# Four new fill-up tiles and one larger one shift where the operands of the expert stage begin in SBUF

## The chip, the cores and the metric

The kernel runs on one core of one Trainium2 chip. The metric is the device time of one execution in microseconds. The kernel before was timed in 3 runs; a further execution was taken with the hardware profiler.

## The reference, cut to what matters

Attention gives 4608 rows of 512 numbers, and a mixture of 8 experts is applied to them. The logits pick one expert per row; the expert is two matrix products with a ReLU between:

```python
out_up = np.repeat(sm_attn(q_d, k_d, v_d), 4, axis=2)      # coarse attention over means of 4 positions
out_local = ...                                            # softmax over keys with |i - j| < 4
x = (out_up + out_local).transpose(0, 2, 1, 3).reshape(4608, 512)
expert_idx = np.argmax(x @ w_gate, axis=1)                 # 8 experts, gate_w = softmax probability
for e in range(8):
    h = np.maximum(x_sorted[lo:hi] @ w1[e], 0.0)           # 512 -> 1024
    y_sorted[lo:hi] = h @ w2[e]                            # 1024 -> 512
return gate_w[:, None] * y_sorted[inv_perm]
```

q, k and v are 8 batches x 8 heads x 576 positions x 64.

## The kernel before, in words

**Attention, to about 239 us.** 32 pairs of heads go through a hand-written list of steps, `PASS`. In it TensorE multiplies plain float32 operands (each such matmul stands in the trace as two) and transposes float32 tiles with the identity `ident` of the tile `cf`. Finished rows are scattered to a DRAM table `xs`, one region per expert.

**Experts, from about 239 us to the end** (expert 0 starts earlier, between the last steps of attention). Each operand is split in a high and a low part (`w1h`, `w1l`, `xh`, `xl`, `w2h`, `w2l`, `hh`, `hl`), all float32r, and a product is three matmuls: high by high, high by low, low by high. A matmul has a stationary operand, loaded into the array by a weight load of 128 columns (engine PEld in the trace), and a moving operand that streams through, mostly 512 columns.

- `s1(e, f)`, lines 587 to 600: for block f of 128 of the 1024 hidden units, 12 matmuls into one bank; stationary `w1` tiles, moving `xh0`/`xl0` (512 tokens). Expert 0 does it in two parts of 256 tokens.
- `s2(e, t)`, through `down`, lines 602 to 612: for a tile t of 128 tokens, 24 matmuls; stationary `hh`/`hl`, moving `w2`, 8 tiles f.
- The rows past 512 of an expert go through `full` (stationary `xh1`/`xl1` with moving `w1`, then stationary `thh`/`thl` with moving `w2`) or, when at most 64 are left, `half` (stationary `xb` and `tb`). In this data each of the two is run 4 times. Which one is decided on the chip by a count, in `rest_of`.

**Where tiles lie.** Every tile pool here keeps its tiles one behind the other in the order in which their names are first used, each size rounded up to a multiple of 32 bytes per partition. `wpool` and, behind it, `mp[0]` lie on the left and grow upward; `mp[1]` lies at the upper end of the right side and `wodd` below it, so what is added to one of them moves its first tiles down. A tile that is only there to take up room is made by `home`, which also writes zeros to it with a memset on GpSimd. The tiles that the matmuls read, all of sizes that are multiples of 256 bytes, begin at these addresses modulo 256:

| tiles | pool | before |
|---|---|---|
| `w1` of even experts | `wpool` | 224 |
| `xh0`, `xl0`, `hh`, `hl` | `mp[0]` | 224 |
| `w2`, f = 0 to 5 | `mp[0]` | 224 |
| `w2`, f = 6, 7; `xh1`, `xl1`, `xb`, `thh`, `thl`, `tb` | `mp[1]` | 224 |
| `w1` of odd experts | `wodd` | 224 |

The slices that matmuls take of them begin at multiples of 256 bytes too. So, in the kernel before, the distance modulo 256 from a moving to a stationary operand is 0 in each matmul of the expert stage. In attention the distances vary from matmul to matmul: the stationary `XT` of the transposes (line 444) begins at 64, 80, 96 and 112 for even pairs of batches and at 128 to 176 for odd ones, with the moving identity always at 0; the moving `AT` of line 337 begins at 32 or 64 for alternating pairs of heads and steps by 208 within them, with the stationary `vw` always at 96.

The engines' queues in the expert stage: ScalarE and VectorE split the next weights and evacuate banks, GpSimd casts the rows' indices and issues the indirect DMAs of the outputs (line 616), SyncE the loads.

## Time and profile before

| | |
|---|---|
| median of 3 runs | 669.18 us (665.74 to 670.09) |
| profiled execution | 662.55 us, of which the span of its instructions is 660.6 us |
| mean granted TensorE clock | 0.992 |
| TensorE matmuls busy | 625.5 us (95%) |
| weight loads busy (beside matmuls) | 510.3 us (77%) |
| VectorE, ScalarE, GpSimd busy | 371.9, 320.0, 216.3 us |

[...] How much time a matmul takes up is read from the starts of two that follow each other; this text calls that its pitch. Start times stand with two decimals of a microsecond, so a pitch is best read over many.

### The profile page before, as it was taken

Reading aid. Unit: us, or ns where it says so; the run is one execution under the profiler, and the core shown is the slowest. Engines: PE = TensorE matmul, PEld = TensorE weight load, DVE = VectorE, ACT = ScalarE, POOL = GpSimd, SP = SyncE. Lnnn points to the kernel's source line nnn. Section 1 sums busy time; section 2 is a strip of 40 time slices with the busy share of each in tenths; the row PEclk is TensorE's granted clock in tenths of the full one; section 3 lists DMA queues with packets and bytes.
Section 4 is the critical chain, followed back from the end, with each engine's and each line's share of the span. In section 5 each row is a group of like instructions: output and inputs, shape, how many; then the busy total and the mean of one; then the engine's idle time right before and its main releaser. Section 6 shows DMA issues by size and latency. Waiting matters only on the chain.

```text
span 660.6 us, 15650 instructions
## 1 busy us (share of the span) xinstructions
PE 625.5 (95%) x6163; PEld 510.3 (77%) x6163; DVE 371.9 (56%) x691; ACT 320.0 (48%) x845; POOL 216.3 (33%) x316
## 2 busy tenths in 40 slices
PE   7988998999998989999999999999999989999994
PEld 3766776777776978888888888888888878888873
DVE  5968899999996646382373065166128247115020
ACT  3656777778785535362362254254236145224120
POOL 6955887888770611101101011101110101110111
PEclk9989999999999989999999999999999999999998
DMA  9999999899534496284176238238228528110001
GB/s 305 286 270 264 291 280 279 261 281 269 170 128 124 150 297 193 63 232 147 52 182 187 66 133 233 65 94 216 99 80 224 178 77 209 48 46 1 33 18 41
DMA packets 66226, 108.52 MB, mean 164 GB/s; under 512 B 15388, under 2 KB 36524, under 8 KB 66112
## 3 DMA queue, kind: packets, MB, share of 16 engines
q1 hardware_dynamic: 59840, 87.62, 47.8%
q0 software_dynamic: 5984, 19.01, 7.9%
q8 instruction: 66, 1.08, 0.7%
q10 hardware_dynamic: 288, 0.42, 0.2%
q14 instruction: 48, 0.39, 0.2%
HBM read 86.98 MB, written 23.67 MB: 167 GB/s over the span
## 4 chain that ended last, share of the span: by engine, by line
PE 68%; issue 10%; DVE 10%; DMA 4%; POOL 3%; ACT 2%; SPq 1%; POOLq 0%; another core or an unknown queue 0%; DVEq 0%; ACTq 0%
PE p L596 8%; PE p L597 8%; PE p L595 8%; PE p L611 7%; PE p L609 7%; PE p L610 7%; PE pD L285 3%; PE pPV L337 2%; PE pX L322 2%; PE pX L691 2%; PE pX L710 2%; DMA vd<-in_vd_dram 2%; PE pPV L350 1%; DVE A L271 1%; PE pS L236 1%
## 5 line engine op out<-in xcount | busy, mean ns | idle before, releaser
L595 PE MATMUL p<-xh,w1h 128*128 128x512 f32 (+1 forms) x288 | 106.7, 370 | 3.2 <-issue 1.9
L616 POOL DMA_INDIRECT out_dram<-y,tix x39 | 38.0, 974 | 212.9 <-ACT y L628 201.5
L596 PE MATMUL p<-xl,w1h 128*128 128x512 f32 (+1 forms) x288 | 106.0, 368 | 0.8 <-DVE xl L543 0.8
L597 PE MATMUL p<-xh,w1l 128*128 128x512 f32 (+1 forms) x288 | 105.9, 368 | 0.0
L609 PE MATMUL p<-w2h,hh 128*128 128x512 f32 x256 | 101.1, 395 | 0.0
L611 PE MATMUL p<-w2h,hl 128*128 128x512 f32 x256 | 99.8, 390 | 0.0
L610 PE MATMUL p<-w2l,hh 128*128 128x512 f32 x256 | 99.6, 389 | 0.0
L600 DVE SCALAR_TENSOR_TENSOR hl<-p,hh 128x512 fp32r<-128x512 f32 (+1 forms) x72 | 45.5, 632 | 93.3 <-ACT hh L599 91.3
L599 ACT ACTIVATE hh<-p 128x512 fp32r<-128x512 f32 (+1 forms) x72 | 39.6, 551 | 78.9 <-PE p L597 78.9
L628 ACT ACTIVATE y<-p,gi 128x512 f32<-128x512 f32 x32 | 22.0, 689 | 93.8 <-PE p L611 89.4
L595 PEld LDWEIGHTS p<-xh,w1h 128*128 128x128 f32 x288 | 55.0, 191 | 13.1 <-issue 2.3
L596 PEld LDWEIGHTS p<-xl,w1h 128*128 128x128 f32 x288 | 55.1, 191 | 9.7 <-DVE xl L543 0.9
L597 PEld LDWEIGHTS p<-xh,w1l 128*128 128x128 f32 x288 | 55.0, 191 | 8.7
L611 PEld LDWEIGHTS p<-w2h,hl 128*128 128x128 f32 x256 | 48.0, 188 | 10.2
L610 PEld LDWEIGHTS p<-w2l,hh 128*128 128x128 f32 x256 | 48.1, 188 | 9.6
L609 PEld LDWEIGHTS p<-w2h,hh 128*128 128x128 f32 x256 | 48.1, 188 | 9.4
L471 POOL DMA_INDIRECT xs<-xr,ix x36 | 36.8, 1021 | 42.0 <-ACT w1h L181 12.4
L182 DVE TENSOR_TENSOR w1l<-raw,w1h 128x512 fp32r<-128x512 f32 (+1 forms) x72 | 49.4, 686 | 0.8
L299 ACT ACTIVATE AD<-pD,mxd 128x144 f32<-128x144 f32 x96 | 35.3, 376 | 19.1 <-DVE A L271 18.8
L543 DVE TENSOR_TENSOR xl<-pX,xh 128x512 fp32r<-128x512 f32 x38 | 24.7, 684 | 35.2 <-ACT xh L542 34.2
L585 DVE TENSOR_TENSOR w2l<-raw,w2h 128x512 fp32r<-128x512 f32 x64 | 43.4, 681 | 1.1 <-ACT w2h L584 0.6
L216 POOL TENSOR_TENSOR vdt<-vd 72x512 f32<-72x512 f32 x32 | 40.8, 1276 | 6.4 <-DMA vd<-in_vd_dram 4.2
(148 smaller groups left out, 1204.7 us busy)
## 6 DMA issues: line engine op xcount, KB each, us to landing
raw<-in_w_dram SPq DMA_DIRECT2D x64, 512.0 KB
qk<-in_qk_dram SPq DMA_DIRECT2D x32, 583.0 KB
vw<-in_vw_dram SPq DMA_DIRECT2D x32, 320.0 KB
vd<-in_vd_dram SPq DMA_DIRECT2D x32, 288.0 KB
xrow<-xs SPq DMA_DIRECT2D x32, 192.0 KB
xrow<-xs SPq DMA_DIRECT2D x32, 128.0 KB
xs<-zs SPq DMA_DIRECT2D x6, 512.0 KB
xs<-pad SPq DMA_DIRECT2D x3, 257.0 KB
```

What stands on the lines that cost most here:

```text
L182: nc.vector.tensor_sub(lo[:, s], src[:, s], hi[:, s])
L216: nc.gpsimd.tensor_add(t2, v[:, 0:2], v[:, 2:4])
L585: nc.vector.tensor_sub(lo, src, hi)
L595: nc.tensor.matmul(p, wh[:, fs], xh[:, k, r], start=(k == 0), stop=False)
L596: nc.tensor.matmul(p, wh[:, fs], xl[:, k, r], start=False, stop=False)
L597: nc.tensor.matmul(p, wl[:, fs], xh[:, k, r], start=False, stop=(k == 3))
L599: nc.scalar.activation(hh[:, f, r], p, AF.Relu)
L600: nc.vector.scalar_tensor_tensor(hl[:, f, r], p, 0.0, hh[:, f, r], op0=OP.max, op1=OP.subtract)
L609: nc.tensor.matmul(p, hh, wh, start=(f == 0), stop=False)
L610: nc.tensor.matmul(p, hh, wl, start=False, stop=False)
L611: nc.tensor.matmul(p, hl, wh, start=False, stop=(f == 7))
L616: ins = nc.gpsimd.indirect_dma_start(out=out, out_offset=bass.IndirectOffsetOnAxis(ap=ix, axis=0), in_=y, in_offset=None, bounds_check=N - ...
```

## The change

`home` gets the pool as an argument and is defined earlier. Four new fill-up tiles are made, and one grows:

- `gap2`, 64 bytes in `wpool` ahead of `w1h0`;
- `gap3`, 192 bytes at the head of `mp[0]`;
- `gap`, from 64 to 96 bytes in `mp[0]`, ahead of `w2`;
- `gap1`, 160 bytes behind the last tile of `mp[1]`;
- `gap4`, 64 bytes behind the last tile of `wodd`.

```diff
+    def home(name, n, pl):
+        nc.gpsimd.memset(pl.tile([128, n], F32, name=name), 0.0)
...
         if (e, k) not in W1:
             pl = wpool if e % 2 == 0 else wodd[0]
+            if (e, k) == (0, 0):
+                home("gap2", 16, wpool)
             W1[e, k] = (pl.tile([128, F], F32R, name=f"w1h{k}"), pl.tile([128, F], F32R, name=f"w1l{k}"))
+            if (e, k) == (1, 3):
+                home("gap4", 16, pl)
...
         if (e, f) == (0, 0):
-            home("tgi", 2)
-            home("ttix", 1)
-            home("gap", 16)
+            home("tgi", 2, mp[0])
+            home("ttix", 1, mp[0])
+            home("gap", 24, mp[0])
...
             mp["th", 1] = [mp[1].tile([128, 8, 2, HALF], F32R, name="tb")]
+            home("gap1", 40, mp[1])
...
             _, mp["p1"] = pool(name="psM1", bufs=2, space=PSUM)
+            home("gap3", 48, mp[0])
             x_load(0, 0)
```

No matmul, load or other instruction is added, removed or moved but the memsets of the four new tiles.

## Rows read from the trace of the kernel before

**Rows 1.** The page, part 1: engine, busy us (share of the span), instructions.

```profile
PE 625.5 (95%) x6163; PEld 510.3 (77%) x6163; DVE 371.9 (56%) x691; ACT 320.0 (48%) x845; POOL 216.3 (33%) x316
```

**Rows 2.** The chain of waits that ended last, by engine and by line.

```profile
PE 68%; issue 10%; DVE 10%; DMA 4%; POOL 3%; ACT 2%; SPq 1%; POOLq 0%; another core or an unknown queue 0%; DVEq 0%; ACTq 0%
PE p L596 8%; PE p L597 8%; PE p L595 8%; PE p L611 7%; PE p L609 7%; PE p L610 7%; PE pD L285 3%; PE pPV L337 2%; PE pX L322 2%; PE pX L691 2%; PE pX L710 2%; DMA vd<-in_vd_dram 2%; PE pPV L350 1%; DVE A L271 1%; PE pS L236 1%
```

**Rows 3.** A stretch, mostly expert 1: busy us by engine, granted clock, DMA share, GB/s.

```profile
268.00:313.00 45.00, 45.00 (x200) 37.24 (x200) 22.74 (x36) 19.66 (x35) 6.65 (x13) 1.00 0.52 149
```

**Rows 4.** Groups by line and shape, TensorE: count | busy us, mean ns | idle before.

```profile
L609 PE MATMUL p<-w2h,hh 128*128 128x512 f32 x256 | 101.1, 395 | 0.0
...
L595 PE MATMUL p<-xh,w1h 128*128 128x512 f32 x224 | 87.3, 390 | 1.9 <-issue 1.9
...
L595 PE MATMUL p<-xh,w1h 128*128 128x256 f32 x64 | 19.4, 304 | 1.3 <-ACT xh L542 1.2
...
L691 PE MATMUL pX<-w1h,xb 128*128 128x512 f32 x32 | 12.5, 392 | 0.4 <-DVE xb L730 0.4
```

**Rows 5.** Timeline of TensorE, two ends of the stretch of rows 3: start, us.

```profile
268.04 0.39 PE L710 MATMUL pX<-w2h,tb 128*128 128x512 f32 x1
...
312.92 0.39 PE L691 MATMUL pX<-w1h,xb 128*128 128x512 f32 x1
```

**Rows 6.** Timelines of matmuls and of weight loads, one instant.

```profile
421.13 0.39 PE L610 MATMUL p<-w2l,hh 128*128 128x512 f32 x1
...
421.14 0.19 PEld L611 LDWEIGHTS p<-w2h,hl 128*128 128x128 f32 x1
```

**Rows 7.** Eight bf16 matmuls of 512 columns in attention: timeline, and busy time by stretch.

```profile
13.02 1.90 PE L136 MATMUL pPV<-wsrc 128*128 128x512 bf16 x8
...
13.00:15.00 2.00, 2.00 (x12) 0.79 (x10) 1.76 (x4) 0.33 (x2) 1.59 (x2) 1.00 1.02 297
```

**Rows 8.** Expert 0, 256 columns: a stretch's granted clock, and timeline at either clock.

```profile
240.30:242.90 2.60, 2.60 (x15) 2.60 (x14) 0.59 (x2) 0.90 (x2) 1.43 (x4) 0.50 1.03 411
...
241.13 0.41 PE L596 MATMUL p<-xl,w1h 128*128 128x256 f32 x1
241.35 0.41 PE L597 MATMUL p<-xh,w1l 128*128 128x256 f32 x1
...
245.82 0.28 PE L596 MATMUL p<-xl,w1h 128*128 128x256 f32 x1
...
247.74 0.28 PE L597 MATMUL p<-xh,w1l 128*128 128x256 f32 x1
```

**Rows 9.** Timeline of TensorE after a pause of 0.43 us, expert 7.

```profile
632.28 0.40 PE L691 MATMUL pX<-w1l,xb 128*128 128x512 f32 x1
...
632.75 0.40 PE L691 MATMUL pX<-w1l,xb 128*128 128x512 f32 x1
632.99 0.39 PE L691 MATMUL pX<-w1h,xb 128*128 128x512 f32 x1
...
634.60 0.39 PE L691 MATMUL pX<-w1l,xb 128*128 128x512 f32 x1
```

**Rows 10.** Timeline of attention: blocks of lines 337 and 444, from several passes.

```profile
65.74 0.81 PE L337 MATMUL pPV<-AT,vw 64*64 64x58 f32 x40
66.48 0.66 PE L444 MATMUL pX<-cf,XT 128*128 128x128 f32 x4
72.03 0.81 PE L337 MATMUL pPV<-AT,vw 64*64 64x58 f32 x40
...
132.79 0.66 PE L444 MATMUL pX<-cf,XT 128*128 128x128 f32 x4
```

**Rows 11.** Groups by line, GpSimd.

```profile
L616 POOL DMA_INDIRECT out_dram<-y,tix x39 | 38.0, 974 | 212.9 <-ACT y L628 201.5 <-DVE y L714 11.1 <-issue 0.3
...
L470 POOL MEMSET spacer<- 1x1 f32 x36 | 3.2, 88 | 0.1
...
L575 POOL MEMSET gap<- 128x16 f32 x1 | 0.1, 142 | 0.0
```

## The prediction, made before the change was timed

> **What bounds the kernel now.** Read the page's first part, then the chain of waits. Matmuls fill 95% of the span [rows 1], and PE is 68% of the chain, the six lines of `s1` and `down` 45% of the span alone [rows 2]; the other engines are at 56% or less. In the expert stage it is sharper: in 45 us TensorE is busy for 45.00 us, at the full granted clock, with the DMAs at 0.52 [rows 3]. Nothing there waits for data. So the stage lasts as long as its matmuls' pitch times their number, and this change can act on it only through that pitch.

> The number: groups of 512 columns are three of 256 (as the first of [rows 4]), three of 224, and ten of 32 (as the last), 768 + 672 + 320 = 1760; of 256 columns there are three of 64, 192.

> The pitch: between the two rows of [rows 5] lie 44.88 us and 198 matmuls (of the 200 that [rows 3] counts, the first and the last begin outside), so 0.2267 us each. 1760 x 0.2267 = 399 us: **a nanosecond of pitch is 1.76 us**, and 1% of the time (6.7 us, about what a measurement of this kernel can tell from no change) is 3.8 ns.

> **What the pitch holds.** The next weights are read while the present operand streams: L611's load starts 0.01 us behind L610's matmul and takes 0.19 us [rows 6]. Two reads of SBUF run together, and the change moves just their addresses. Is there anything to gain? The bf16 matmuls of 512 columns stand at (1.90 - 0.39) / 7 = 0.2157 us, also at clock 1.00 (0.39 us is the last one's own duration, taken from [rows 5]) [rows 7]. The float32r ones take 11.0 ns more. [...]

> **The change part by part.** The new starts, modulo 256, by adding the fill-ups to the layout table: even `w1` 224 + 64 = 32. `mp[0]` 224 + 64 + 192 = 224 again, so `x` and `h` stay. `w2` f < 6 gains 64 + 192 + 32 = 288, so 0. `mp[1]` moves down by 160, to 64. `wodd` moves down by 160 + 64, to 0. Distances of stationary less moving: `s1` even 32 - 224 = 64, odd 32; `s2` f < 6 224, f >= 6 160; the tails 32 or 64, and 0 where `thh`, `thl` or `tb` meet `w2` f >= 6 (4 x 6 and 4 x 4, 40 of 1760 matmuls).

> *Pitch at the new distances.* The trace of before has no float32r matmul at a distance other than 0, so I bound it. From below: 0.2157, the bf16 row; 1720 x 11.0 + 152 x 10 = 20.4 us less (of the 192 narrow matmuls some 40 lie at half clock or among attention's, which I leave out). From above: after a pause the pitch isn't settled; from 632.28 to 634.60 ten matmuls take 0.232 each, one of them 0.24 [rows 9], and settle to 0.2267 only then. At distance 0 throughout, the same matmuls can thus cost 5.3 ns more: 1760 x 5.3 = 9.3 us more if they never settled. Between the ends I take the nearest rows where distance does vary. The stationary-moving distance of L337 differs by 32 between one pass and the next, and both blocks of 40 last 0.81 us; transposes with `XT` at 64 to 112 and at 128 to 176 both last 0.66 us per four [rows 10]. Neither shows an address. These rows are plain float32 and not the same mode, but they are the only ones with two distances: I take **0 us**.

> [...]

> *The memsets.* Four more on GpSimd, each at 0.14 us as the `gap` of before [rows 11], 0.6 us in all. `gap2` falls in the attention loop, ahead of scatters; `gap3` at its end, ahead of the last of them, where it waits for readers of `qk` that ran a pass earlier; `gap1` and `gap4` in expert 0, where GpSimd's outputs wait 201.5 us for `y` in all [rows 11]. That idle time is the cover of the last two; without it they would cost 0.3 us. The first two delay pooling or scatter by 0.3 us at most. I cost all at 0, at most 0.6.

> *Moved tiles.* Attention's left tiles move by 64 bytes as one; [rows 10] say that this is free. The DMAs and evacuations keep sizes and order. 0.

> **The sum** is 0 against the profiled execution: 662.55 us, of which 660.6 are the span. That execution is 6.6 us (1.0%) under the median of 669.18, and one of the runs is at 665.74; medians of three of this kernel can thus move by some 3 us with nothing changed. I take 668, just under the median.

> **The rivals.** *Faster: the reads collide at distance 0.* The same place modulo 256 in both streams is where a collision would be expected, and the extra appears when both run at the full clock, not at half [rows 8]. Against it: [rows 10], and that five different distances would all have to be better. If all lose the 11 ns, 668 - 20.4 = 647.6 us; with half of it, 657.8. It decides from a mean pitch below 0.2229.

> *Slower: distance 0 is the settled state, and others hold the matmuls in the unsettled one.* Place: each of the float32r matmuls; price as above, 668 + 9.3 = 677.3 us. For it: [rows 9] show that a matmul with the same addresses and shape costs 0.24 or 0.2267 depending on how the reads stand in time, and shifting addresses shifts that. Against: after each pause it settles within some ten matmuls, and other distances may settle as well. It decides from a mean pitch above 0.2305.

> *The change doesn't do what it says*: a fill-up lies elsewhere than I worked out and the distances remain 0, or a whole class does. Then the time is 668 too. It is 4 in 100 of the case of no change.

> **How the numbers follow.** No change 0.43 (668, own range 663 to 673). Faster 0.34: the extra at full clock is real and needs a cause, and two streams of addresses in step are one. Slower 0.23: the same sensitivity with the other sign. Range: 651 leaves out the last sixth of the gain, where every class would have to reach the bf16 row; 678 takes in the whole price of the slower case with little beyond. About 1 in 10 is left out. Over 1% faster 0.34, within 1% 0.43, over 1% slower 0.23.

> **What would show it.** Timelines of `s1` of an even and an odd expert and of `down`, f < 6 against f >= 6. The forecast: 0.2267 in all four, as in [rows 5]. The faster rival: 0.216 to 0.223 in most classes, while the 40 matmuls left at 0 keep 0.2267. The slower one: 0.230 and more in long stretches without a pause. A class at one value and its neighbour at another would prove that the distance acts, whatever the sum. The forecast is wrong if any of the four moves by over 4 ns with the time following; it would then fail at the step that takes plain float32 rows for float32r.

## The result, and the profile after

The changed kernel takes 673.83 us (median of 11 runs, 670.95 to 678.98) against 666.36 for the kernel before (11 runs): a ratio of 1.0113, 95% interval 1.0089 to 1.0137. In a second comparison it was 1.0148 (1.0104 to 1.0192). It is slower, by 1.1% in the first comparison and 1.5% in the second, the case to which the prediction gave 0.23. The time lies in the stated range; the forecast of no change was wrong.

The profiled execution after takes 673.9 us, its span 672.0, against 660.6. The page's first part, as in [rows 1]:

```profile
PE 636.8 (95%) x6160; PEld 511.4 (76%) x6163; DVE 371.5 (55%) x691; ACT 319.9 (48%) x845; POOL 216.1 (32%) x320
```

TensorE has the same matmuls (three records are missing) and is busy for 11.3 us more. Weight loads are busy for 1.1 us more, all others within 0.5 us of before; GpSimd has its four memsets more. The same stretch length as in [rows 3], at the same granted clock, and the groups that answer to [rows 4]:

```profile
274.00:319.00 45.00, 45.00 (x199) 36.31 (x198) 22.55 (x37) 20.03 (x37) 5.71 (x11) 1.00 0.52 147
```

```profile
L612 PE MATMUL p<-w2h,hh 128*128 128x512 f32 x256 | 102.3, 400 | 0.0
...
L598 PE MATMUL p<-xh,w1h 128*128 128x512 f32 x224 | 89.3, 399 | 1.9 <-issue 1.9
```

The mean of one goes from 395 to 400 ns and from 390 to 399 ns, with idle time ahead of them unchanged. So nothing waits longer; the matmuls themselves take up more. Own durations overlap: a matmul of 0.39 us is followed by the next one's start after some 0.23. So the pitch is read from starts in the timeline. These are the first and the last matmul of `s1` in expert 1, in expert 2, and of the first token tile of `s2` in expert 1:

```profile
271.61 0.39 PE L598 MATMUL p<-xh,w1h 128*128 128x512 f32 x1
293.77 0.40 PE L600 MATMUL p<-xh,w1l 128*128 128x512 f32 x1
...
324.73 0.39 PE L598 MATMUL p<-xh,w1h 128*128 128x512 f32 x1
346.89 0.39 PE L600 MATMUL p<-xh,w1l 128*128 128x512 f32 x1
...
294.00 0.40 PE L612 MATMUL p<-w2h,hh 128*128 128x512 f32 x1
299.36 0.39 PE L614 MATMUL p<-w2h,hl 128*128 128x512 f32 x1
```

`s1` is 96 matmuls, so 95 pitches: 22.16 / 95 = 0.2333 us at distance 32 (expert 1) and 0.2333 at distance 64 (expert 2). The tile of `s2` has 24: 5.36 / 23 = 0.2330. Before it was 0.2267 [rows 5].

By class, as means of the gaps between starts (those under 0.26 us, which leaves pauses out), in ns:

| class | distance before, after | matmuls | pitch before | after | change, us |
|---|---|---|---|---|---|
| `s1`, 512 columns | 0; 64 and 32 | 672 | 226.7 | 233.2 | 4.4 |
| `s2` | 0; 224 and 160 | 768 | 227.5 | 233.1 | 4.3 |
| tails, up products | 0; 32 and 64 | 160 | 227.2 | 233.2 | 1.0 |
| tails, down products | 0; 64, and 0 where f is 6 or 7 | 160 | 227.1 | 232.7 | 0.9 |
| `s1` of expert 0, 256 columns at full clock | 0; 64 | 165 | 119.6 | 117.2 | -0.4 |

In `s2` the tiles f < 6, at distance 224, and f = 6 and 7, at 160, both take 233.1.

The 40 matmuls of the tails that the layout leaves at distance 0 don't keep 226.7: they average 230.8, the other down products 233.3. They come four or six at a time behind matmuls at 64. These are the first and the last of such a six:

```profile
380.16 0.39 PE L612 MATMUL pX<-w2h,thh 128*128 128x512 f32 x1
381.31 0.39 PE L614 MATMUL pX<-w2h,thl 128*128 128x512 f32 x1
```

1.15 / 5 = 0.230, with single gaps of 0.226 to 0.235, much as in the first matmuls after a pause [rows 9]. So what a matmul takes up depends also on those ahead of it; a settled pitch is read over many at one distance.

The sum of the table is 10.2 us of the 11.4 by which the spans differ. The rest, 1.2 us, is no more than what is lost at expert 6: in both executions TensorE pauses there for some 2 us (1.89 before, 1.95 after), and in the one after the granted clock then stands at 0.50 for a stretch. From the timeline and the busy time by stretch:

```profile
536.71 0.40 PE L600 MATMUL p<-xh,w1l 128*128 128x512 f32 x1
539.05 0.50 PE L598 MATMUL p<-xh,w1h 128*128 128x512 f32 x1 [1.95 <-issue]
...
540.63 0.63 PE L598 MATMUL p<-xh,w1h 128*128 128x512 f32 x1
541.05 0.63 PE L599 MATMUL p<-xl,w1h 128*128 128x512 f32 x1
541.48 0.63 PE L600 MATMUL p<-xh,w1l 128*128 128x512 f32 x1
...
543.19 0.63 PE L598 MATMUL p<-xh,w1h 128*128 128x512 f32 x1
```

```profile
540.70:543.60 2.90, 2.90 (x8) 2.23 (x7) 0.82 (x2) 1.45 (x3) 0.00 (x0) 0.50 0.00 0
```

Seven matmuls at 0.43 us instead of 0.23 are 1.4 us. Seven such are in the trace of the first experiment below, where every distance is 0 (mean granted clock 0.985), and none in that of the third (`s2` alone, 0.990) or in a second trace of the changed kernel (0.990); so this comes and goes and isn't the change's.

### The profile page after: what moved, and what is told of

Same layout as the page of the kernel before. It is cut to its first block, busy times and chain, and to the rows that moved or that the text cites. A ratio compares the mean times of both kernels' runs of the same rounds, so it can differ in the third digit from the quotient of the medians.

```text
span 672.0 us, 15650 instructions
## 1 busy us (share of the span) xinstructions
PE 636.8 (95%) x6160; PEld 511.4 (76%) x6163; DVE 371.5 (55%) x691; ACT 319.9 (48%) x845; POOL 216.1 (32%) x320
## 4 chain that ended last, share of the span: by engine, by line
PE 69%; issue 10%; DVE 7%; POOL 5%; DMA 4%; ACT 2%; SPq 1%; POOLq 0%; another core or an unknown queue 0%; DVEq 0%; ACTq 0%
PE p L599 8%; PE p L598 8%; PE p L600 8%; PE p L613 7%; PE p L612 7%; PE p L614 7%; PE pD L292 3%; PE pX L329 2%; PE pPV L344 2%; PE pX L695 2%; PE pX L714 2%; PE pPV L357 2%; PE pS L243 2%; DMA vd<-in_vd_dram 2%; POOL xs L478 1%
## 5 line engine op out<-in xcount | busy, mean ns | idle before, releaser
L598 PE MATMUL p<-xh,w1h 128*128 128x512 f32 (+1 forms) x288 | 108.6, 377 | 3.1 <-issue 1.9
L599 PE MATMUL p<-xl,w1h 128*128 128x512 f32 (+1 forms) x288 | 108.0, 375 | 0.8 <-DVE xl L550 0.8
L600 PE MATMUL p<-xh,w1l 128*128 128x512 f32 (+1 forms) x288 | 107.8, 374 | 0.0
L613 PE MATMUL p<-w2l,hh 128*128 128x512 f32 x256 | 101.2, 395 | 0.0
```

The lines of the kernel that those rows point to most:

```text
L598: nc.tensor.matmul(p, wh[:, fs], xh[:, k, r], start=(k == 0), stop=False)
L599: nc.tensor.matmul(p, wh[:, fs], xl[:, k, r], start=False, stop=False)
L600: nc.tensor.matmul(p, wl[:, fs], xh[:, k, r], start=False, stop=(k == 3))
L613: nc.tensor.matmul(p, hh, wl, start=False, stop=False)
```

## The experiments

The theory after the result: **what counts is the distance modulo 256 between the stationary and the moving operand; at 0 the matmuls reach a settled pitch of 0.2267, at another they don't.** Rivals: the place of a tile or pool counts, not the distance; the memsets or the moved tiles cost elsewhere; one class alone carries it; the cost depends on how far the distance is, with a better place than 0 somewhere.

**All operands moved together.** All fill-ups are made, each distance stays 0.

```diff
-            home("gap3", 48, mp[0])
+            home("gap3", 64, mp[0])
...
-            home("gap", 24, mp[0])
+            home("gap", 16, mp[0])
...
-            home("gap1", 40, mp[1])
+            home("gap1", 48, mp[1])
...
-                home("gap4", 16, pl)
+                home("gap4", 64, pl)
```

> All four fill-ups are made, but in sizes (64, 256, 64, 192 and 256 bytes) that put every operand of the expert stage at 32 modulo 256, so that each distance is 0 as before while every tile has moved and every new memset is there. If the distance between the two operands is what costs: pitch 0.2267 us in s1 and down, and the time of before (ratio 0.997 to 1.003). If the place itself counts, of a tile or of a pool: pitch near 0.233 and ratio near 1.011. If it is the memsets: pitch 0.2267 and ratio near 1.011.

665.22 us against 665.82; ratio 0.999 (0.9956 to 1.0023). `s1` of expert 1, its two ends:

```profile
274.47 0.39 PE L598 MATMUL p<-xh,w1h 128*128 128x512 f32 x1
296.00 0.39 PE L600 MATMUL p<-xh,w1l 128*128 128x512 f32 x1
```

21.53 / 95 = 0.2266. At this other place the pitch is that of before, and the memsets cost nothing that can be told from 0: of the rivals, those of the place and of the memsets are out. By the layout the distances of `s1` are odd multiples of 256 bytes in even experts and even multiples in odd ones in the kernel before, and the other way round here; all take 0.2267, so the remainder by 256 is what to look at.

The half clock comes here too. From the timeline, six matmuls apart, and the busy time by stretch:

```profile
536.18 0.63 PE L599 MATMUL p<-xl,w1h 128*128 128x512 f32 x1
538.74 0.63 PE L599 MATMUL p<-xl,w1h 128*128 128x512 f32 x1
...
536.10:539.10 3.00, 3.00 (x8) 2.30 (x7) 0.00 (x0) 0.55 (x2) 0.00 (x0) 0.50 0.02 5
```

2.56 / 6 = 0.427 at distance 0, and between 540.63 and 543.19 of the changed kernel, at 64, 2.56 / 6 as well: at half the clock the two distances take the same.

**The two halves of the change.** `s1` alone (with the up products of the tails): `gap` back to 64 bytes, no `gap1`, `gap4` of 224 bytes.

```diff
-            home("gap", 24, mp[0])
+            home("gap", 16, mp[0])
...
-            home("gap1", 40, mp[1])
...
-                home("gap4", 16, pl)
+                home("gap4", 56, pl)
```

> Distances 64 and 32 in s1 as in the changed kernel; hidden to output products (down, in s2 and in the tails) back at 0; the up products of the tails at 192 and 224. By the distance, term by term: s1 at 0.2332, down at 0.227, and 672 x 6.5 + 160 x 6.3 ns less some 130 x 2.4 for expert 0's narrow matmuls = 5.1 us, ratio 1.008. If only the moving weights of down matter, or what they do to their neighbours: ratio 1.000.

`s2` alone (with both products of the tails): no `gap2`, no `gap3`, `gap4` of 96 bytes.

```diff
-            if (e, k) == (0, 0):
-                home("gap2", 16, wpool)
...
-                home("gap4", 16, pl)
+                home("gap4", 24, pl)
...
-            home("gap3", 48, mp[0])
```

> The other half: s1 at distance 0, down of s2 at 224 and 160 as in the changed kernel, up products of the tails at 96. By the distance, term by term: s1 at 0.2267, down at 0.2331, 768 x 5.8 + 280 x 6.3 ns = 6.2 us, ratio 1.009. If the cost sits in s1 alone: ratio 1.000. The two halves should add to the whole (10.4 us by the pitches of the changed kernel's trace).

Of the kernel with `s1` alone, the ends of `s1` and of the first tile of `s2` in expert 1; then the same of the kernel with `s2` alone:

```profile
271.54 0.39 PE L598 MATMUL p<-xh,w1h 128*128 128x512 f32 x1
293.71 0.40 PE L600 MATMUL p<-xh,w1l 128*128 128x512 f32 x1
...
293.94 0.39 PE L612 MATMUL p<-w2h,hh 128*128 128x512 f32 x1
299.16 0.39 PE L614 MATMUL p<-w2h,hl 128*128 128x512 f32 x1
```

```profile
274.04 0.39 PE L596 MATMUL p<-xh,w1h 128*128 128x512 f32 x1
295.61 0.39 PE L598 MATMUL p<-xh,w1l 128*128 128x512 f32 x1
...
295.84 0.40 PE L610 MATMUL p<-w2h,hh 128*128 128x512 f32 x1
301.20 0.39 PE L612 MATMUL p<-w2h,hl 128*128 128x512 f32 x1
```

0.2334 and 0.2270 in the first, 0.2271 and 0.2330 in the second: each class follows its own distance and none its neighbour's. The times: 1.0038 (1.0005 to 1.0072) and 1.0094 (1.0056 to 1.0132). The second is what its terms gave; the first is below its 1.008, just outside the interval. By the pitches of its own trace it would be some 4.2 us, 1.006, which the interval holds: expert 0's narrow matmuls gave back 0.9 us instead of 0.3, and the tails' up products cost 4.1 ns a matmul instead of 6.3. Those of even experts stand at distance 192, and in their three tails of 128 rows the matmuls behind the first three settle at 0.229. One of the three, its fourth and its last matmul:

```profile
363.46 0.39 PE L666 MATMUL pX<-w1h,xh 128*128 128x512 f32 x1
368.04 0.40 PE L668 MATMUL pX<-w1h,xl 128*128 128x512 f32 x1
```

4.58 / 20 = 0.229, which the next experiments find for 192 in `s1` too. Together the two times make 1.013, which the intervals of the whole hold.

**The distances one by one.** Each expert takes its x tiles at another offset in a slightly longer tile, so one execution shows up to eight distances in `s1`, with all else at 0. Each of these kernels, and the one after them, was run once; only pitches within an execution are read from them.

```diff
+STEP = (0, 4, 8, 16, 24, 32, 40, 48)
...
-                XH[e, c] = tuple(mp[c].tile([128, 4, FIRST if c == 0 else 128], F32R, name=f"x{w}{c}") for w in "hl")
+                XH[e, c] = tuple(
+                    mp[0].tile([128, 4 * FIRST + 64], F32R, name=f"x{w}0")[:, STEP[e]:STEP[e] + 4 * FIRST].rearrange("p (k t) -> p k t", k=4)
+                    if c == 0 else mp[1].tile([128, 4, 128], F32R, name=f"x{w}1") for w in "hl")
```

> The kernel before with the x tiles of expert e begun 0, 16, 32, 64, 96, 128, 160 and 192 bytes into a slightly longer tile, so that s1 stands at distance 0, 240, 224, 192, 160, 128, 96 and 64 for experts 0 to 7 and all else at 0. If any distance but 0 loses the settled state: 0.233 in s1 of experts 1 to 7 alike. If the cost is graded by distance, or has a shorter period: values that differ by expert, with 128 back at 0.2267 if the period is 128, and 240 back at it if nearness counts. If 0 is not the best place: one of them below 0.2267.

With `STEP = (48, 60, 62, 63, 2, 1, 12, 56)`:

> The scan of the x tiles again, at the distances 64, 16, 8, 4, 248, 252, 208 and 32 in s1 of experts 0 to 7. Graded by distance: the values of 4, 8 and 16 bytes on either side lie between 0.2267 (at 0) and 0.2333 (at 64), rising with the distance on both sides alike, with 240 at 0.2316 as measured. All or nothing: 0.2333 from 4 bytes on, on both sides. A better place than 0: one of them below 0.2267. Expert 0's 256-column matmuls at 64: 0.1133 as in the kernel with s1 alone changed, or 0.1175 as in the changed kernel.

With `STEP = (16, 52, 44, 36, 28, 20, 61, 16)`:

> The scan's last distances: 192, 48, 80, 112, 144, 176, 12 and 192 for experts 0 to 7. 192 gave 0.2291 in expert 3, alone among the far ones: if that is the distance, expert 7 shows 0.229 again; if it was how that expert's matmuls happened to start, 0.233. The rest 0.233 to 0.234 if far distances are all alike, and below 0.2267 nowhere.

The pitch of `s1` at 512 columns, from its two ends as above (for expert 6, which holds the pause, as the mean of gaps under 0.26 us), in ns:

| distance | pitch | distance | pitch | distance | pitch |
|---|---|---|---|---|---|
| 0 | 226.7 | 64 | 233.3 | 176 | 231.1 |
| 4 | 230.0 | 80 | 231.0 | 192 | 229.1, 229.1 |
| 8 | 232.6 | 96 | 234.2 | 208 | 233.3 |
| 12 | 238.7 | 112 | 233.3 | 224 | 233.4 |
| 16 | 233.3 | 128 | 233.3 | 240 | 231.6 |
| 32 | 233.3 | 144 | 231.1 | 248 | 233.4 |
| 48 | 234.7 | 160 | 233.5 | 252 | 237.4 |

Three pairs of rows behind it: expert 3 of the first scan (192), experts 3 and 5 of the second (4 and 252), expert 7 of the third (192 again).

```profile
383.51 0.40 PE L598 MATMUL p<-xh,w1h 128*128 128x512 f32 x1
405.27 0.39 PE L600 MATMUL p<-xh,w1l 128*128 128x512 f32 x1
```

```profile
383.84 0.39 PE L598 MATMUL p<-xh,w1h 128*128 128x512 f32 x1
405.69 0.39 PE L600 MATMUL p<-xh,w1l 128*128 128x512 f32 x1
...
491.92 0.40 PE L598 MATMUL p<-xh,w1h 128*128 128x512 f32 x1
514.47 0.40 PE L600 MATMUL p<-xh,w1l 128*128 128x512 f32 x1
```

```profile
592.99 0.40 PE L598 MATMUL p<-xh,w1h 128*128 128x512 f32 x1
614.75 0.39 PE L600 MATMUL p<-xh,w1l 128*128 128x512 f32 x1
```

21.76 / 95 = 0.2291 twice, in another expert, on another place in time: at 512 columns 192 has a value of its own. Neither of the simple pictures holds. It isn't all or nothing (192 and 4 cost a third to a half of the usual 6.6 ns, 252 and 12 cost 11 and 12), and it isn't nearness to 0 either (252 is 4 bytes away and among the worst). No distance of these 20 is below 0.2267, and 128 isn't back at it, so among the 21 tried 0 stands alone.

**One matmul of three off 0.** In even experts `w1l` lies 64 further, in odd ones `xl`.

```diff
-                XH[e, c] = tuple(mp[c].tile([128, 4, FIRST if c == 0 else 128], F32R, name=f"x{w}{c}") for w in "hl")
+                XH[e, c] = tuple(
+                    mp[0].tile([128, 4 * FIRST + (64 if w == "l" else 0)], F32R, name=f"x{w}0")[:, o:o + 4 * FIRST].rearrange("p (k t) -> p k t", k=4)
+                    if c == 0 else mp[1].tile([128, 4, 128], F32R, name=f"x{w}1")
+                    for w, o in (("h", 0), ("l", 48 if e % 2 else 0)))
...
+                his = [pl.tile([128, F], F32R, name=f"w1h{j}") for j in range(4)]
+                if e == 0:
+                    nc.gpsimd.memset(pl.tile([128, 16], F32, name="gapa"), 0.0)
+                los = [pl.tile([128, F], F32R, name=f"w1l{j}") for j in range(4)]
...
```

> The kernel before with one operand shifted in s1: in even experts w1l stands 64 further, so that of the three matmuls of a k the first two have their own pair at 0 and the third (w1l with xh) at 64; in odd experts xl does, so that the second alone (w1h with xl) is at 64. The load that runs beside a matmul is the next one's. If the pair that counts is a matmul's moving operand with the next one's weights: in even experts the second of the three is long (xl beside the load of w1l), the first and the third short; in odd experts the second. If it is a matmul's own pair: in even experts the third. If one matmul of three off 0 unsettles the whole sequence: all three near 0.233. If a third of them counts singly: a mean of 0.2267 + 0.0066 / 3 = 0.2289.

Experts 1 and 2, the two ends of `s1`:

```profile
271.83 0.39 PE L608 MATMUL p<-xh,w1h 128*128 128x512 f32 x1
293.58 0.39 PE L610 MATMUL p<-xh,w1l 128*128 128x512 f32 x1
...
323.83 0.39 PE L608 MATMUL p<-xh,w1h 128*128 128x512 f32 x1
345.77 0.40 PE L610 MATMUL p<-xh,w1l 128*128 128x512 f32 x1
```

0.2289 in odd experts, as if one of three counted singly, but 0.2309 in even ones, as if two did. Matmul by matmul, the gaps after the first, second and third are 228.3, 229.1 and 235.7 ns in even experts: the third, whose own pair is off 0, is long. In odd experts, where the second's own pair is off, they are 229.4, 229.4 and 228.3: it isn't. So whether a matmul's own pair counts, or its moving operand with the next one's weights, is **left open**.

**The changed kernel once more, and expert 0 alone at 64.** The first repeats the comparison. The second is the scan's kernel with one entry off 0:

```diff
+STEP = (48, 0, 0, 0, 0, 0, 0, 0)
```

> The changed kernel once more, since its matmuls' pitches sum to 10.1 us over the kernel before and its ratio of 1.0113 [1.0089, 1.0137] to 7.5 us. If the pitch is all of it and holds in each execution: ratio near 1.015, and the first interval was low by chance. If something gives back 2 to 3 us in executions that are not profiled, or the settled state of before isn't reached in each: again 1.010 to 1.012.

1.0148 (1.0104 to 1.0192); 10.2 us would be 1.015. This interval holds it, the first one, up to 1.0137, doesn't. A part of the gap can be the granted clock. Over the executions for which it is listed, the mean span is 7.8 us longer after (17 executions) than before (40), but the mean clock is 0.988 after and 0.986 before, and among the 40 an execution with 0.01 less is longer by some 5.6 us. At the same clock the difference is thus an estimated 9 us. Why the clocks differ, and whether the last microsecond is real, is left open.

> All distances 0 as before, but for expert 0's x tiles, which stand at 64: its 192 matmuls of 256 columns took 0.120 us at 0 and 0.113 to 0.118 at 64. If that holds: 0.113 to 0.118 there, 0.2267 in the rest, 0.3 to 1.0 us less, ratio 0.9985 to 0.9995, which these rounds may not tell from 1. If the narrow ones were shorter for what ran beside them: 0.120 and ratio 1.000.

666.73 us against 666.96, ratio 1.0004 (0.9976 to 1.0031). Two matmuls of expert 0 with 24 between them, in this kernel, in the first trace of the changed kernel and in the second:

```profile
244.93 0.28 PE L600 MATMUL p<-xh,w1l 128*128 128x256 f32 x1
...
247.76 0.28 PE L598 MATMUL p<-xh,w1h 128*128 128x256 f32 x1
```

```profile
247.39 0.28 PE L600 MATMUL p<-xh,w1l 128*128 128x256 f32 x1
...
250.33 0.28 PE L598 MATMUL p<-xh,w1h 128*128 128x256 f32 x1
```

```profile
247.82 0.28 PE L600 MATMUL p<-xh,w1l 128*128 128x256 f32 x1
...
250.66 0.28 PE L598 MATMUL p<-xh,w1h 128*128 128x256 f32 x1
```

2.83 / 25 = 0.113, 2.94 / 25 = 0.118 and 2.84 / 25 = 0.114, where it was 0.120 [rows 8]. The narrow matmuls are shorter off 0, but at 64 they settle at one of two values: the changed kernel shows 0.118 here in one execution and 0.113 in another, the second scan, also at 64, 0.118, and within an execution stretches of either follow each other. So at 256 columns the distance alone doesn't fix the pitch, and what chooses between the two is open. 182 x 5 ns = 0.9 us is too little to show in these times. No version that is measurably faster than the kernel before came out.

## Why the prediction was wrong

**What bounds the stage** was right: the stage is its matmuls' pitch times their number, and the four long classes make 10.6 us of the difference at 6 ns each.

**The pitch at the new distances** is the step that failed. The bounds, -20.4 and +9.3 us, nearly held what came, about 10.2 by the pitches. The value taken between them was 0, from transposes and plain float32 matmuls in attention that show no address [rows 10]. The runs put in its place: in float32r matmuls of 512 columns each of 20 other distances costs 2 to 12 ns over 226.7, and 233.3 is the commonest value. That rows of another mode show nothing was no evidence for this one. They differ in more than the mode: they are 58 and 128 columns wide, and each block of line 337 runs through many distances in steps of 208, so that two blocks shifted by 32 could last alike even if single matmuls differed. [Rows 7] and [rows 8] had the better hint. At clock 1.00 a float32r matmul of 512 columns takes 11.0 ns more than a bf16 one, 0.2267 us against 0.2157; one of 256 takes 0.120, where half of the gap of 0.22 at clock 0.50 is 0.110. A cost that shows in one mode has to be looked for in that mode. What the 11.0 ns at distance 0 are is still open: at 512 columns none of the 20 other distances took them away. The lower bound also takes 10 ns off each of 152 narrow matmuls. That term is the author's estimate from the 0.110, and no run shows it; the runs showed 0.120 us at distance 0 and 0.118 or 0.113 at 64.

**The slower rival** was right in place and sign, and near in price: the matmuls of 512 columns, 0.232 forecast from the ten after a pause [rows 9], 0.233 measured; +9.3 us forecast, 10.2 by the pitches. The price is in part luck: it fits the distances that the change happens to make, while others of the scan cost 2 or 12 ns. What spoke against it, that other distances may settle as well, holds in part: at the distances seen in several experts (0, 32, 64 and 192) the mean is fixed to 0.1 ns in each kernel, though single gaps in it go on alternating (after the change, in expert 1, means of 0.238, 0.232 and 0.230 after the first, second and third matmul of a k). They settle too, at a worse value; that they are held in the state of after a pause, or that addresses shift how the reads stand in time, is not shown.

**The faster rival** fell with the scan. Its argument, that streams in step at 0 collide, was the author's guess: it has the sign wrong for 512 columns, and only for 256 columns, at distance 64, is the sign right, by 2 to 7 ns. No run shows a collision of reads.

**That the change doesn't do what it says** is out: each class moved with the distance that the layout gives.

**The memsets and moved tiles** cost nothing that can be told from 0: 0.999 (0.9956 to 1.0023) with all of them in place at distance 0. **The remark on medians**, that they move by some 3 us by themselves, was about right: the kernel before gave 665.82, 666.36 and 666.96 as medians of its comparisons, 669.18 in its first three runs.

## What to carry to other kernels

## What the runs showed that was not expected

- The pitch differed with the distance between operands, down to 4 bytes: 226.7 ns at 0, 230.0 at 4, 237.4 at 252, 238.7 at 12, 229.1 at 192, 233.3 at nine others within 0.2.
- The sign turns with the width: at distance 64, 512 columns take 6.6 ns more than at 0, and 256 columns 2 or 6 to 7 less (0.118 or 0.113 against 0.120), with both values in one kernel.
- At a granted clock of 0.50 nothing of it is seen: 512 columns take 0.427 us at distance 0 and at 64.
- A few matmuls at 0 behind others off 0 don't settle: the 40 of the tails average 230.8 ns.
